# Attention and a squared-ReLU feed-forward on one core: all engines in written order, weight rounding in single hops, value products in one run

## The chip, the cores and the metric

The kernel runs on one core of one Trainium2 chip. The metric is the device time of one execution in microseconds (us). Five runs of the kernel before gave 1637.34 to 1641.2 us, median 1638.19. A core has TensorE (PE; its weight loads are shown as PEld), VectorE (DVE), ScalarE (ACT), GpSimd (POOL) and SyncE (SP), which here only issues transfers. Each has an instruction stream of its own.

## What is computed

```python
# q, k, v: (8, 12, 448, 64) float32; w_in (768, 2048), w_out (2048, 768): 64-bit floats
def rmsnorm(x, g):
    return x / np.sqrt(np.mean(x * x, axis=-1, keepdims=True) + 1e-06) * g
scores = np.matmul(rmsnorm(q, g_q), rmsnorm(k, g_k).transpose(0, 1, 3, 2)) / np.sqrt(64)
attn = softmax(scores)                      # row maximum taken off, sums plus 1e-09
x = np.matmul(attn, v)                      # then (B,H,S,D) -> (3584, 768)
g = np.maximum(x @ w_in, 0.0) ** 2
out = g @ w_out                             # (3584, 768) float32
```

## The kernel before

The program looks at the gains first: if the scores can't grow large, it takes `attention_then_ffn_bounded`, which needs no row maximum. Only that branch runs on these inputs and only it is spoken of.

**Attention.** Two heads of one batch make a *pair*; there are 8 x 6 = 48. The 448 rows of a head are cut into NJ = 4 chunks of SP = 112. For a pair i, `load` and `load_v` bring q, k and v; `norm` squares on ScalarE, sums on DVE, then takes the root's inverse (the power, L535) and scales (L537) on POOL into `qkn`; `transposes` turns `qkn` on TensorE into two PSUM tiles `pt`, which ScalarE copies into `qkT` with the gains; `scores` computes one chunk of scores transposed (`sc`) and its exp on ScalarE (`pr`); `values` multiplies chunks of `pr` with v into `pav`, and `sums` multiplies `pr`, or with `pe_sums` off the sum `acc` of the four chunks, with ones into `tot`; `finish` takes the reciprocal of `tot` (L601) and writes `pav` times it into `xT` (L602). For the second batch of a span it also makes the differences `xC` (L607 to L612).

**Feed-forward.** Two batches are one *span*; there are four. Each of the two products of a span is done by seven products of half-size blocks in place of eight (Strassen's way in Winograd's form): the weights' blocks A11, A12, A22 and their combinations S1 to S4 lie ready in DRAM (`w1s`, `w2s`), the data's combinations are made on DVE: `xC` in `finish`, `gC` in `combine` (four subtractions for each of HF = 8 values f). `first_product` goes through f = 0..7; each f has seven *units* (yields) of one half-size product, accumulated in the PSUM tiles `pa`, `pb`, `pc`, `pd` and added up on DVE (`z`, `y`, `g22`, `g21`, `g12`), with ReLU on ScalarE and the square on POOL or ScalarE (`activate`). `second_product` yields after each matmul; a group of eight fills a PSUM tile `ps`, which DVE adds up into `p1`, `y`, `ct`; `deliver` transposes a finished `ct` into `po`, and ScalarE and SP bring it out.

**Weights.** They arrive as 64-bit floats and are turned to 32 bits in the kernel, 32 chunks of 128x768 (n = 0..31, half for each matrix), two making the seven blocks of one f. `make_w(n, step)` has four steps: 0, exponent on DVE (L451) and two Relus on ScalarE (L453, L454); 1, sign (L457), mask (L458) and low word (L459) on DVE, then a Copy on ScalarE (L460); 2, two products on POOL (L467) and for an odd n the four combinations (L471 to L474); 3, for an odd n the blocks are written to DRAM. Raw words and blocks lie in the buffers of `gC` and in parts of `gT` and of a spare pool, which the data needs later. `weights(upto)` makes whole *ticks*: in tick n, step 0 of chunk n, step 1 of n - 1, step 2 of n - 2 and step 3 of n - 3, all issued at one place, and then the loads of raw chunks whose place is free.

**Order.** The main part runs: attention of span 0 with 14 ticks spread over it; first product of span 0 with ticks to 29; attention of ALONE = 3 pairs of span 1 with the last ticks; `combine` for all f; then for each span its second product, interleaved with the attention of the next span (its remaining pairs), and the next first product. `attention` has two places per pair where other work is put in (yields): the values of a pair are split, chunks 0 and 1 behind its own scores 2 and 3, chunks 2 and 3 behind scores 0 and 1 of the next pair, where `finish` stands as well. The last line of the listing's branch says who sets the order: TensorE and SP execute in written order, while DVE, ScalarE and POOL get an order from a planner at build time.

**PSUM.** `ps_s` has two tiles of two banks (`sc`), `ps_o` one each of `o` (`pav`) and `t` (`tot`, and `pa`), `ps_m` two (`pt`, `pb`, `pc`, `pd`, `ps`, `po`).

Of the kernel before, what the change touches and what calls it, by code (L numbers as in the profile page):

```python
# [9 lines left out]
F32 = mybir.dt.float32  # L10
# [294 lines left out]
def attention_then_ffn_bounded(  # L305
# [132 lines left out]
    def make_w(n, step):  # L438

        if not 0 <= n < 2 * NFC:  # L440
            return
        b = [blocks_of(n)[:, i] for i in range(8)]

        at = (S2, A22)[n % 2]
        e = blocks_of(n)[:, at:at + 2].rearrange("p k m -> p (k m)")
        eu = e.bitcast(U32)
        words = words_of(n)
        low, high = pairs_of(words)
        f = low.bitcast(F32)
        if step == 0 and doubles:  # L450
            nc.vector.tensor_scalar(eu, high, 20, 0x7FF, ALU.logical_shift_right, ALU.bitwise_and)  # L451

            nc.scalar.activation(e, eu, AF.Relu, bias=clamp1, scale=-1.0)  # L453
            nc.scalar.activation(eu, e, AF.Relu, bias=clamp2, scale=-(2.0 ** 23))  # L454
        if step == 1 and doubles:

            nc.vector.scalar_tensor_tensor(eu, high, 0x80000000, eu, ALU.bitwise_and, ALU.bitwise_or)  # L457
            nc.vector.tensor_scalar(high, high, 0xFFFFF, None, ALU.bitwise_and)  # L458
            nc.vector.scalar_tensor_tensor(f, low, 2.0 ** -32, high, ALU.mult, ALU.add)  # L459
            nc.scalar.activation(f, f, AF.Copy, bias=1.0, scale=2.0 ** -20)  # L460
        if step == 2:

            to = ((A11, A12), (A21, A22)) if n < NFC else ((A11, A21), (A12, A22))
            for half, blk in enumerate(to[n % 2]):
                part = slice(half * HW, (half + 1) * HW)
                if doubles:
                    nc.gpsimd.tensor_tensor(b[blk], f[:, part], e[:, part], ALU.mult)  # L467
                else:
                    nc.gpsimd.tensor_copy(b[blk], words.bitcast(F32)[:, part])
        if step == 2 and n % 2:  # L470
            nc.gpsimd.tensor_tensor(b[S1], b[A21], b[A22], ALU.add)  # L471
            nc.gpsimd.tensor_tensor(b[S2], b[S1], b[A11], ALU.subtract)
            nc.gpsimd.tensor_tensor(b[S3], b[A11], b[A21], ALU.subtract)
            nc.gpsimd.tensor_tensor(b[S4], b[A12], b[S2], ALU.subtract)  # L474
        if step == 3 and n % 2:
# [8 lines left out]
            written[0] = n + 1  # L484

    written = [0]
# [22 lines left out]

    qks, vs, qkTs, probs, pavs, tots, accs, normed = {}, {}, {}, {}, {}, {}, {}, {}  # L510
# [14 lines left out]
    def norm(i):  # L525
# [8 lines left out]
        nc.gpsimd.tensor_scalar(rflat, rflat, 1.0 / D, 1e-6, ALU.mult, ALU.add)  # L534
# [9 lines left out]
    def transposes(i):  # L544
        qkn = normed.pop(i)
        qkT = loads.tile([P, 2, S], F32, tag="qkT", name="qkT")
        for s in range(2):
            pt = ps_m.tile([P, S], F32, tag="m", name="pt")
            for j in range(NJ):
                nc.tensor.transpose(pt[:, j * SP:(j + 1) * SP],  # L550
                                    qkn[:, s, j].rearrange("p h d -> p (h d)"), ident[:SP, :SP])
            nc.scalar.activation(qkT[:, s], pt, AF.Copy, scale=gains[:, s:s + 1])  # L552
        qkTs[i] = qkT

    def scores(work, i, c, pe_sums):
# [10 lines left out]
        if c == 0 or pe_sums:  # L566
            pass
        elif c == 1:
            accs[i] = work.tile([SP, 2, S], F32, tag="acc", name="acc", bufs=1)
            nc.gpsimd.tensor_tensor(accs[i], probs[i, 0], pr, ALU.add)  # L570
        else:
            (nc.vector if c == 2 else nc.gpsimd).tensor_tensor(accs[i], accs[i], pr, ALU.add)
# [3 lines left out]
    def values(i, cs, pe_sums):  # L576
        if 0 in cs:
            pavs[i] = ps_o.tile([P, S], F32, tag="o", name="pav")
        for c in cs:
# [6 lines left out]
        if not pe_sums and NJ - 1 in cs:  # L586
# [8 lines left out]
    def finish(work, i):  # L595


        b, hp = divmod(i, NPAIR)
        t = b % 2
        rec = work.tile([P, S], F32, tag="rec", name="rec", bufs=1)  # L600
        nc.vector.reciprocal(rec, tots.pop(i))  # L601
        nc.vector.tensor_tensor(xT[:, t, hp], pavs.pop(i), rec, ALU.mult)  # L602
        del vs[i]
        if t:
# [9 lines left out]
    def attention(work, first, end, pe_sums):  # L614

        last = (first // (2 * NPAIR) + 1) * 2 * NPAIR
        for i in range(first, end):
            if i + 3 < min(last + 2, B * NPAIR):
                load(i + 3)
            scores(work, i, 0, pe_sums)  # L620
            scores(work, i, 1, pe_sums)
            if i + 2 < last:
                norm(i + 2)
            if i > first:
                values(i - 1, (2, 3), pe_sums)
                finish(work, i - 1)
            yield
# [4 lines left out]
            scores(work, i, 2, pe_sums)  # L632
            scores(work, i, 3, pe_sums)
            values(i, (0, 1), pe_sums)
            if i == end - 1:
                values(i, (2, 3), pe_sums)
                finish(work, i)
            yield


    def combine(f):
# [5 lines left out]
        sub(gC[:, 0, f], g12, g11, ALU.subtract)  # L647
        sub(gC[:, 1, f], g22, gC[:, 0, f], ALU.subtract)
        sub(gC[:, 2, f], g21, gC[:, 1, f], ALU.subtract)
        sub(g12, g22, g12, ALU.subtract)  # L650

    def first_product(work, span):
# [11 lines left out]
        def activate(g, src):  # L664
            nc.scalar.activation(g, src, AF.Relu)  # L665
            if span == 0 and src is not g:
# [4 lines left out]
        for f in range(HF):  # L671
# [4 lines left out]
            pa = ps_o.tile([P, S], F32, tag="t", name="pa")  # L676
# [242 lines left out]
```

## Time and profile before

| | us |
|---|---|
| five runs, median (lowest to highest) | 1638.19 (1637.34 to 1641.2) |
| the profiled execution | 1633.54 |
| its span, first to last instruction | 1631.7 |
| first attention: first scores to last sums | 18.3 to 198.6 |
| first product of span 0, to the end of its matmuls | to 334.4 |
| three pairs alone, to the first matmul of the second product | to 386.28 |

Busy times by these stretches, of PE, PEld, DVE, ACT and POOL (number of instructions), then the granted TensorE clock, the share of the DMA engines and GB/s:

```profile
18.30:198.60 180.30, 142.41 (x664) 55.88 (x664) 119.75 (x107) 105.72 (x130) 135.12 (x109) 0.91 0.51 159
198.60:334.40 135.80, 131.35 (x344) 65.35 (x344) 76.62 (x94) 59.89 (x87) 84.62 (x78) 0.97 0.74 241
334.40:386.30 51.90, 39.62 (x178) 15.37 (x177) 36.79 (x40) 26.04 (x34) 42.74 (x33) 0.87 0.58 180
386.30:600.00 213.70, 204.11 (x743) 92.32 (x741) 81.86 (x86) 54.19 (x73) 84.47 (x50) 1.00 0.28 82
600.00:1631.70 1031.70, 999.86 (x3240) 478.31 (x3240) 319.86 (x398) 225.28 (x334) 317.47 (x232) 1.00 0.30 88
```

Some groups of instructions, with their count, busy time, mean ns of one, and the idle time of the engine before them with what ended most of it:

```profile
L601 DVE RECIPROCAL rec<-tot 128x448 f32<-128x448 f32 x48 | 141.9, 2956 | 231.8 <-PE tot L593 231.8
L535 POOL TENSOR_TENSOR rstd<-rstd,mhalf 112x16 f32<-112x16 f32 x48 | 140.5, 2927 | 3.8
L582 PE MATMUL pav<-pr,vt 112*64 112x448 f32 x768 | 179.6, 576 | 41.1 <-issue 33.7
L570 POOL TENSOR_TENSOR acc<-pr 112x896 f32<-112x896 f32 x33 | 68.5, 2076 | 86.6 <-PE tot L593 79.3
```

A timeline row gives start, duration, engine, line, operation, output and inputs, shape and count; in brackets stands the engine's idle time before it and what ended it.

### The profile page before, as it was taken

How to read it: one execution, taken by the hardware profiler on the slowest of the kernel's cores; microseconds unless marked ns; L12 is line 12 of the kernel's file. 1: busy time of each engine (PE TensorE's matmuls, PEld its weight loads, DVE VectorE, ACT ScalarE, POOL GpSimd, SP SyncE). 2: the span in 40 equal slices, each digit the busy share in tenths (PEclk: the TensorE clock that was granted, in tenths of full speed). 3: DMA queues.
4: the chain of work that ended last, by engine and by line, in shares of the span. 5: the costliest groups of instructions: out<-in, count | busy, mean ns of one | idle time of the engine just before them, and what ended most of it. 6: DMA issues, size and time to landing. Idle time of an engine off the chain costs nothing.

```text
span 1631.7 us, 14479 instructions
## 1 busy us (share of the span) xinstructions
PE 1519.3 (93%) x5172; PEld 708.6 (43%) x5172; DVE 638.1 (39%) x729; ACT 475.8 (29%) x661; POOL 672.1 (41%) x516
## 2 busy tenths in 40 slices
PE   4688799978999999999999999999999999999998
PEld 2233354533444445554444445554444445555444
DVE  4556846576333333333333332333333342332001
ACT  5456435463232311123233311123332311211000
POOL 5967737685434402235554421225555320221000
PEclk9799899989999999999999999999999999999999
DMA  5345367864232233333232313333233213333332
GB/s 170 108 150 187 121 225 261 249 216 126 74 96 85 79 88 89 98 88 96 85 90 81 100 56 99 88 96 97 85 90 92 71 56 91 87 87 95 102 105 63
DMA packets 157717, 180.37 MB, mean 111 GB/s; under 512 B 10692, under 2 KB 134084, under 8 KB 157636
## 3 DMA queue, kind: packets, MB, share of 16 engines
q1 hardware_dynamic: 157636, 179.35, 36.4%
q8 instruction: 43, 0.70, 0.2%
q14 instruction: 38, 0.31, 0.1%
HBM read 146.28 MB, written 33.03 MB: 110 GB/s over the span
## 4 chain that ended last, share of the span: by engine, by line
PE 82%; DVE 5%; POOL 3%; ACT 3%; issue 3%; DMA 3%; SPq 1%; DVEq 0%; POOLq 0%; ACTq 0%
PE ps L733 31%; PE sc L561 8%; PE pav L582 8%; PE pa L661 8%; PE pd L661 8%; PE pc L661 8%; PE pb L661 4%; PE tot L593 4%; PE pt L550 2%; ACT qkT L552 1%; DMA words<-in_moe_w_out_dram 1%; DMA qk<-in_k_dram 1%; POOL gC L467 1%; DVE ct L747 1%; POOL qkn L537 1%
## 5 line engine op out<-in xcount | busy, mean ns | idle before, releaser
L733 PE MATMUL ps<-gT,sw 128*128 128x448 f32 x768 | 306.6, 547 | 7.1 <-DVE ct L747 3.6
L669 POOL TENSOR_TENSOR gT<-gT 128x448 f32<-128x448 f32 x120 | 115.2, 960 | 376.1 <-ACT gT L665 376.1
L733 PE MATMUL ps<-gC,sw 128*128 128x448 f32 x576 | 230.6, 546 | 4.0 <-ACT osb L725 2.0
L601 DVE RECIPROCAL rec<-tot 128x448 f32<-128x448 f32 x48 | 141.9, 2956 | 231.8 <-PE tot L593 231.8
L564 ACT ACTIVATE pr<-sc 112x896 f32<-112x896 f32 x192 | 166.8, 914 | 191.3 <-PE sc L561 191.3
L582 PE MATMUL pav<-pr,vt 112*64 112x448 f32 x768 | 179.6, 576 | 41.1 <-issue 33.7
L733 PEld LDWEIGHTS ps<-gT,sw 128*128 128x128 f32 x768 | 141.0, 190 | 157.2 <-issue 141.4
L561 PE MATMUL sc<-qkT 64*112 64x448 f32 x768 | 173.6, 570 | 7.8 <-ACT pr L564 7.1
L661 PE MATMUL pa<-xT,sw 128*128 128x448 f32 x384 | 157.2, 546 | 3.0 <-DVE rec L601 3.0
L733 PEld LDWEIGHTS ps<-gC,sw 128*128 128x128 f32 x576 | 106.1, 190 | 118.3 <-issue 110.5
L535 POOL TENSOR_TENSOR rstd<-rstd,mhalf 112x16 f32<-112x16 f32 x48 | 140.5, 2927 | 3.8
L665 ACT ACTIVATE gT<-gT 128x448 f32<-128x448 f32 x96 | 55.1, 575 | 291.6 <-DVE gT L693 183.1
L534 POOL TENSOR_SCALAR rstd<-rstd 112x16 f32<-112x16 f32 x48 | 32.6, 680 | 242.0 <-DVE rstd L533 241.1
L582 PEld LDWEIGHTS pav<-pr,vt 112*64 112x64 f32 x768 | 50.8, 143 | 153.8 <-issue 147.6
L552 ACT ACTIVATE qkT<-pt,gains 128x448 f32<-128x448 f32 x96 | 58.7, 632 | 170.9 <-PE pt L550 170.9
L725 ACT COPY osb<-po 112x512 f32<-112x512 f32 x48 | 28.1, 586 | 275.5 <-PE po L723 275.5
L661 PEld LDWEIGHTS pa<-xT,sw 128*128 128x128 f32 x384 | 73.4, 192 | 74.6 <-issue 70.6
L537 POOL TENSOR_TENSOR qkn<-qk,rstd 112x512 f32<-112x512 f32 x96 | 103.5, 1100 | 3.6
L570 POOL TENSOR_TENSOR acc<-pr 112x896 f32<-112x896 f32 x33 | 68.5, 2076 | 86.6 <-PE tot L593 79.3
L533 DVE TENSOR_REDUCE rstd<-qkn 112x16 f32<-112x1024 f32 x48 | 58.1, 1211 | 115.8 <-ACT qkn L530 115.6
L561 PEld LDWEIGHTS sc<-qkT 64*112 64x112 f32 x768 | 61.4, 174 | 89.0 <-issue 65.3
L550 PE MATMUL pt<-ident,qkn 112*128 112x112 f32 x384 | 53.7, 271 | 37.2 <-ACT qkT L552 16.7
(82 smaller groups left out, 1650.6 us busy)
## 6 DMA issues: line engine op xcount, KB each, us to landing
sw<-w1s SPq DMA_DIRECT2D x224, 192.0 KB, 2.4
sw<-w2s SPq DMA_DIRECT2D x168, 256.0 KB, 2.7
qk<-in_q_dram SPq DMA_DIRECT2D x48, 224.0 KB, 3.2
qk<-in_k_dram SPq DMA_DIRECT2D x48, 224.0 KB, 3.7
vt<-in_v_dram SPq DMA_DIRECT2D x48, 224.0 KB, 3.0
w1s<-gC SPq DMA_DIRECT2D x8, 1344.0 KB, 6.2
w2s<-gC SPq DMA_DIRECT2D x24, 448.0 KB, 4.6
out_dram<-osb SPq DMA_DIRECT2D x48, 224.0 KB, 2.9
```

The costliest lines, as they stand in the source:

```text
L535: nc.gpsimd.tensor_tensor(rflat, rflat, mhalf, ALU.pow)
L537: nc.gpsimd.tensor_tensor(qkn[:, s].rearrange("p j h d -> p h j d"), qk[:, s].rearrange("p h (j d) -> p h j d", d=D), rstd[:, s].rearrange ...
L550: nc.tensor.transpose(pt[:, j * SP:(j + 1) * SP], qkn[:, s, j].rearrange("p h d -> p (h d)"), ident[:SP, :SP])
L552: nc.scalar.activation(qkT[:, s], pt, AF.Copy, scale=gains[:, s:s + 1])
L561: nc.tensor.matmul(sc[:, h, 0:S], qkT[rows, 1, c * SP:(c + 1) * SP], qkT[rows, 0, :], start=True, stop=True)
L564: nc.scalar.activation(pr, sc[:, :, 0:S], AF.Exp)
L570: nc.gpsimd.tensor_tensor(accs[i], probs[i, 0], pr, ALU.add)
L582: nc.tensor.matmul(pavs[i][h * D:(h + 1) * D, :], vs[i][:, h, c, :], pr[:, h, :], start=(c == 0), stop=(c == NJ - 1))
L601: nc.vector.reciprocal(rec, tots.pop(i))
L661: nc.tensor.matmul(ps, stream[n][:, c], rhs[:, c], start=first and c == 0, stop=c == HC - 1, skip_group_check=not first)
L669: nc.gpsimd.tensor_tensor(g, g, g, ALU.mult)
L733: nc.tensor.matmul(ps, stream[n][:, c % 4], rhs_of[i][:, c], start=c == 0, stop=c == HF - 1)
```

## The change

All engines now run in written order. What was left to the planner is written out:

- `make_w` becomes a generator `prepare(t)` that gives one *hop* at each step, four hops to a tick. Hop 0: sign of chunk t - 1 on DVE, first product of t - 2 on POOL. Hop 1: mask and low word of t - 1, second product of t - 2, S1. Hop 2: Copy of t - 1 on ScalarE, exponent of chunk t on DVE, S2 and S3. Hop 3: the two Relus of chunk t, S4, the write-back of chunk t - 3, and the loads of raw words. `weights(upto)` counts hops.
- Attention that runs alone yields once per pair instead of twice. EARLY, LATE and ALL are 48, 120 and 140 hops: 12 ticks in the first attention (four hops at each pair's yield), 18 in the first product of span 0, 5 in the attention alone, which has ALONE = 2 pairs instead of 3.
- All values of a pair stand in one run behind its scores 2 and 3, and `finish` right behind them. The subtractions of `xC` are a function of their own, `combine_x`, placed in the next pair behind its `norm`. In alone attention, ScalarE's copies of the transposes stand behind the exps (`take_transposes`). Both `pt` tiles are taken before the transposes.
- The sums of probabilities (`acc`) are all on DVE; the scale-add of `norm` moves from POOL to DVE; constants are set on DVE.
- `pa` moves from `ps_o` to `ps_s`; in span 0 the square of `g21` moves to ScalarE; in later spans `combine` of f - 1 is done in two parts between the units of f.
- Only two raw chunks, instead of five, are loaded at the start.

```diff
+    def prepare(t):
...
+        if there(t - 1) and doubles:
+            b, e, eu, low, f, high = parts(t - 1)
+            nc.vector.scalar_tensor_tensor(eu, high, 0x80000000, eu, ALU.bitwise_and, ALU.bitwise_or)
+        if there(t - 2):
+            value(t - 2, 0)
+        yield
+        if there(t - 1) and doubles:
+            nc.vector.tensor_scalar(high, high, 0xFFFFF, None, ALU.bitwise_and)
+            nc.vector.scalar_tensor_tensor(f, low, 2.0 ** -32, high, ALU.mult, ALU.add)
+        if there(t - 2):
+            value(t - 2, 1)
+        total(t - 2, S1, A21, A22, ALU.add)
+        yield
+        if there(t - 1) and doubles:
+            nc.scalar.activation(f, f, AF.Copy, bias=1.0, scale=2.0 ** -20)
+        if there(t) and doubles:
+            b, e, eu, low, f, high = parts(t)
             nc.vector.tensor_scalar(eu, high, 20, 0x7FF, ALU.logical_shift_right, ALU.bitwise_and)
+        total(t - 2, S2, S1, A11, ALU.subtract)
+        total(t - 2, S3, A11, A21, ALU.subtract)
+        yield
+        if there(t) and doubles:
             nc.scalar.activation(e, eu, AF.Relu, bias=clamp1, scale=-1.0)
             nc.scalar.activation(eu, e, AF.Relu, bias=clamp2, scale=-(2.0 ** 23))
...
+        total(t - 2, S4, A12, S2, ALU.subtract)
+        n = t - 3
+        if there(n) and n % 2:
...
+        while loaded[0] <= t + 2 and all(
+                place_of(m) != place_of(loaded[0]) for m in range(max(t - 1, 0), loaded[0])):
+            load_w(loaded[0])
+            loaded[0] += 1
+        yield
...
-        nc.gpsimd.tensor_scalar(rflat, rflat, 1.0 / D, 1e-6, ALU.mult, ALU.add)
+        nc.vector.tensor_scalar(rflat, rflat, 1.0 / D, 1e-6, ALU.mult, ALU.add)
...
+        pts[i] = [ps_m.tile([P, S], F32, tag="m", name="pt") for _ in range(2)]
+        for s, pt in enumerate(pts[i]):
...
+    def take_transposes(i):
+        qkTs[i] = loads.tile([P, 2, S], F32, tag="qkT", name="qkT")
+        for s, pt in enumerate(pts.pop(i)):
+            nc.scalar.activation(qkTs[i][:, s], pt, AF.Copy, scale=gains[:, s:s + 1])
...
+        if c and not pe_sums:
+            nc.vector.tensor_tensor(accs[i], probs[i, 0] if c == 1 else accs[i], pr, ALU.add)
...
-    def attention(work, first, end, pe_sums):
+    def attention(work, first, end, alone):
...
             if i + 2 < last:
                 norm(i + 2)
             if i > first:
-                values(i - 1, (2, 3), pe_sums)
-                finish(work, i - 1)
-            yield
+                combine_x(i - 1)
+            if not alone:
+                yield
             if i + 1 < B * NPAIR:
                 load_v(i + 1)
             if i + 1 < last:
                 transposes(i + 1)
-            scores(work, i, 2, pe_sums)
-            scores(work, i, 3, pe_sums)
-            values(i, (0, 1), pe_sums)
+                if not alone:
+                    take_transposes(i + 1)
+            scores(work, i, 2, alone)
+            scores(work, i, 3, alone)
+            if alone:
+                if i + 1 < last:
+                    take_transposes(i + 1)
+                yield
+            values(i, alone)
+            finish(work, i)
             if i == end - 1:
-                values(i, (2, 3), pe_sums)
-                finish(work, i)
-            yield
+                combine_x(i)
+            if not alone:
+                yield
...
-            pa = ps_o.tile([P, S], F32, tag="t", name="pa")
+            pa = ps_s.tile([P, 2, 512], F32, tag="s", name="pa")[:, 0, 0:S]
...
-    ALONE = 3
-    EARLY, LATE, ALL = 14, 29, 2 * NFC + 3
+    ALONE = 2
+    EARLY, LATE, ALL = 4 * 12, 4 * 30, 4 * (2 * NFC + 3)
...
-        for n in range(WORDS):
-            load_w(n)
+        for _ in range(2):
+            load_w(loaded[0])
+            loaded[0] += 1
...
-                weights(EARLY * (u + 1) // (4 * NPAIR))
+                weights(EARLY * (u + 1) // (2 * NPAIR))
...
-        with tc.manual_schedule(engines={mybir.EngineType.PE, mybir.EngineType.SP}):
+        with tc.manual_schedule():
```

## The prediction

> **What bounds the kernel now.** I read the page's busy shares and its slices first, then the busy time by stretches, then the chain of waits and the timeline inside the stretches where TensorE idles.
>
> ```profile
> span 1631.7 us, 14479 instructions
> ...
> PE 1519.3 (93%) x5172; PEld 708.6 (43%) x5172; DVE 638.1 (39%) x729; ACT 475.8 (29%) x661; POOL 672.1 (41%) x516
> ...
> PE   4688799978999999999999999999999999999998
> ...
> PEclk9799899989999999999999999999999999999999
> ```
>
> TensorE sets the time, and it is full from about the tenth of 40 slices on. What can be won lies in front of that. By stretches (PE, PEld, DVE, ACT, POOL busy, then clock, DMA share, GB/s):
>
> ```profile
> 0.00:100.00 100.00, 62.73 (x282) 25.00 (x283) 53.47 (x52) 53.12 (x65) 72.48 (x67) 0.90 0.43 132
> 100.00:200.00 100.00, 81.61 (x394) 32.22 (x392) 70.90 (x63) 57.26 (x71) 71.60 (x60) 0.93 0.52 167
> 200.00:300.00 100.00, 97.85 (x251) 48.64 (x252) 57.23 (x71) 43.81 (x63) 60.44 (x56) 0.97 0.70 232
> 300.00:400.00 100.00, 86.50 (x319) 38.59 (x318) 68.48 (x83) 47.46 (x65) 68.22 (x56) 0.93 0.64 198
> 400.00:500.00 100.00, 95.59 (x357) 42.55 (x356) 29.88 (x28) 27.37 (x36) 47.65 (x29) 1.00 0.31 90
> ```
>
> The loss is in the first 400 us, the only part with weights to round: stage A, the first attention (first scores at 18.3, last sums end at 198.6), stage B, the first product of span 0 (to 334.4), and stage C, the attention alone (first matmul of the second product at 386.28). From there TensorE is 95% busy or more (stage D). In A a typical idle stretch reads so in the timeline:
>
> ```profile
> 171.06 0.92 PE L593 MATMUL tot<-pr,ones 112*64 112x448 f32 x4
> ...
> 172.19 2.95 DVE L601 RECIPROCAL rec<-tot 128x448 f32<-128x448 f32 x1
> ...
> 175.23 1.22 DVE L533 TENSOR_REDUCE rstd<-qkn 112x16 f32<-112x1024 f32 x1
> ...
> 176.37 0.61 DVE L602 TENSOR_TENSOR xT<-pav,rec 128x448 f32<-128x448 f32 x1
> ...
> 177.08 1.76 PE L582 MATMUL pav<-pr,vt 112*64 112x448 f32 x4 [2.50 <-issue]
> ```
>
> The sums end, DVE takes 2.95 + 0.61 us (here with a reduce of the norm between), and only then is the single `pav` buffer free; in between TensorE has the transposes (0.98) and two scores (1.76), so it idles 2.50 us. "issue" hides the true releaser, xT. All such gaps in A from 18.3 on add up to 37.8 us. Without its gap a pair takes 10.68 us (values at 150.94 and 163.90 are 12.96 apart, gap 2.28; 163.90 to 177.08 gives 13.18 - 2.50). Twelve pairs are 128 us, A lasts 180.3, so some 14 us more are matmuls at a low clock behind gaps (1.76 us for four values where 0.92 is usual).
>
> Stage C hangs on POOL and the write-back of weights:
>
> ```profile
> 376.01 1.73 SPq L481 DMA_DIRECT2D w2s<-gC  x3
> ...
> 382.04 1.16 DVE L647 TENSOR_TENSOR gC<-gT 128x448 f32<-128x448 f32 x2 [5.41 <-DMA w2s<-gC]
> ...
> 385.65 1.73 ACT L564 ACTIVATE pr<-sc 112x896 f32<-112x896 f32 x2 [11.09 <-PE sc L561]
> ...
> 386.28 6.28 PE L733 MATMUL ps<-gT,sw 128*128 128x448 f32 x16
> ```
>
> The last weights leave at 376.01, DVE may overwrite gC from 382.04 (combine), and the second product starts at 386.28, 51.9 after the first product's end.
>
> **The change, stage by stage.**
>
> **A.** Values in one run put scores 0 and 1 (1.76), transposes (0.98) and scores 2 and 3 (1.76) = 4.5 us of TensorE work between the last sums and the next values, where DVE needs 2.95 + 0.61 and two crossings, 3.8. The gap of 2.0 to 3.4 us goes, if nothing else is late. What could be late is the loop that written order ties together: ScalarE's exp 0, exp 1 and Square (0.91 + 0.91 + 1.05), DVE's reduce 1.2 and the small scale-add moved from POOL (0.2 there; I take 0.2), then combine_x, then the hops: sign 1.08, mask 0.9, add 1.25, next exponent 0.75 (means by form from 20 to 200 us, 4.0 together), ScalarE's Copy behind the add and two Relus (0.92 + 1.87), then the next exp 0. Sum with crossings: 10.5. combine_x adds one subtraction (1.0 under POOL's load) in pairs 7 to 9 and three in pairs 10 and 11: 11.5 and 13.5. POOL has per pair 2.97 (power) + 2.45 + 2.26, and 4.4 more every second pair: 9.9 on the mean. So pairs take the longer of 10.7 and this loop: first pair 12.7 as now, six at 11.1 (0.4 for what doesn't overlap), three at 11.7, two at 13.4 = 141; I add 4 for loads of raw weights, which land in 6 to 7 us here. A ends at about 163.5: **-35**. Ends: all eleven later pairs at 10.68 and no wait for loads give -50; the hops at the worst durations of the stage (1.5, 1.3, 1.66, 1.2: 5.7) give 12.2, 13.2, 15.2 a pair and -20; with every second pair another 1 us late at POOL, -14. The twelve ticks replace fourteen in A, so two move to B. On SP the loads and write-backs of hop 3 wait for POOL work one pair older, and qk's loads behind them have a pair of lead: nothing, as long as POOL is under 10.7 a pair. The start doesn't move: constants set by DVE instead of POOL, and gains behind the first norm, all lie before 7.48 us, when the first qk lands, and TensorE's first work at 15.65 waits for POOL's qkn as now; two raw chunks now load ahead of qk(2), which waits for its buffer until 16.5 in any case.
>
> The clock: the stretch from 75 to 80 us shows 0.50 after gaps of 2.56 and 1.99 us, yet after 2.28 us at 163.90 it stays 1.00. Pairs 10 and 11 keep a gap of 2.7 each, which I price by these rows at up to 1.2 us of slow matmuls each; they are counted within the 4 us above. The Trainium skill's "TensorE: Matmul & The Clock Gate" (Part 1) has the half clock come after an idle window of about 3.4 us; by it such gaps would cost nothing beyond themselves, and the sum would be 2 us lower.
>
> **B.** 56 units at 2.2536 us are 126.2; B took 135.8, of it 3.05 waiting for the reciprocal of pair 11 (`pa` shared its buffer with `tot`) and about 3 of low clock. `pa` moves to `ps_s`: the first product starts at once, only `pb`'s third part waits for xC (reciprocal 2.95 + 0.61 + 0.61 against 3.75 of work): 0.7. Transposes in the middle keep 1.3. Eighteen ticks instead of fifteen, nine hops to seven units: two hops fall on units 3 and 6, and where they are exponent and sign, DVE waits for two Relus (1.87) and is then late for z, which must be there one unit (2.25) later. By hand that is two places of about 2 us less some slack: 3. One square for each f of span 0 moves from POOL (0.96) to ScalarE (0.58, idle half of the time between 200 and 300 us): nothing. B: 131.2, **-4.6**; ends -7 (no late z) and +6 (a 2 us wait at every second f and on each of four late loads).
>
> **C.** Two pairs alone instead of three, but five ticks in two lumps. I walk it by hand with the durations of the rows, from B's end E: the Relus of chunk 29 hold exp 0 of pair 12 to E+5; norm, then POOL 2.9 + 2.1 until E+13.6; only then value(28), and SP may load chunk 31 (E+16, lands E+22); DVE's sign for it ends E+27, and in written order the reciprocal of pair 12 stands behind it (E+30.7), the norm of pair 15 behind that, POOL's value(31) and totals behind that (E+43.6); write-back lands E+48.5 (4.8 as now). Queued behind it on DVE are now all 32 subtractions of combine (0.535 apart, 17.1), and behind those the sums of probabilities of pair 14, which TensorE needs: it resumes its dense stream at E+71. Before, TensorE at E+71 (405.4) was ahead of this by ten matmuls of the second product (7.5), a pair's transposes, scores and half its values (5.9) and two scores (1.8): 15.2. **+15**. Ends: +22 if that late load and the write-back each take 3 to 4 us more, +5 if two thirds of combine's 17 us find other TensorE work beside them.
>
> **D.** The probability sums move from POOL (2.08) to DVE (1.08 each, three a pair); reciprocal and combine_x stand before product sums. DVE: 2.95 + 0.61 + 3.24 + 1.4 + 1.2 + 1.1 = 10.5 of the 19.4 us that a pair takes. The cover is DVE's idle time (9.11 before a reciprocal at 756.49); without it each late sum holds a `ps_m` buffer and so the next transposes. In the two pairs per span with three subtractions I find 0.3 to 1.2 us: +2; the wait for POOL's sum at each span's end (0.6, three times) goes: -1. **+1**; ends -2 and +20 (0.6 in each of 34 pairs). In spans 1 to 3 combine in two pieces lies beside 2.25 us units with DVE a third busy: nothing.
>
> **Sum** on the profiled execution (1633.5, span 1631.7): -35 - 4.6 + 15 + 1 = -23.6, 1609.9. The median shown is 1638.2, 4.7 above it: 1638.2 - 23.6 = 1614.6, so 1614.
>
> **Rivals.**
> Combine hides: C costs 2 instead of 15, as DVE's subtractions of free regions run early and TensorE has work. For it: before, some ran at 346 us. Against: written order starts with gC's first region, where the last chunk lies. 1601.
> Rounding binds: DVE and ScalarE hops at their contended worst, A -20.4, B +5, C +15, D +1, +0.6 in all: 1639. For it: DVE and POOL both at 71% in A now. Also here: that the scheduler's order was the written one, which the Relus of rounding between exps at 156 to 163 us speak against.
> Slower: in D the sums queue behind reciprocal or norm, and transposes, which take both `ps_m` buffers, wait. From 0.7 us in each of 34 pairs the gain is used up; at 2 us late less 0.7 slack, 34 x 1.3 = 44: 1658. For it: one buffer held by an unfinished product already costs 0.72 at the transposes of most pairs. Against: DVE's 9 us of slack.
>
> **How the numbers follow.** Forecast 0.55, own range 1603 to 1627; combine hides 0.15; rounding binds 0.16 (0.06 faster, 0.05 the same, 0.05 slower); slower 0.14. Faster 0.76, same 0.05, slower 0.19, at 0.2% (3.3 us), what this measurement can tell. The range 1592 to 1645 takes in the first three and leaves out most of the last and a low tail.
>
> **What would show it.** A: gaps before `pav` under 1 us, pairs 11 to 12 apart, last sums near 163. B: about 131 long, no wait on rec. C: the second product's first matmul 45 to 52 us behind B's end, then an idle TensorE of some 10 us before `tot`, released by DVE's sums behind combine. D: pairs still 19.4 apart. It is wrong if A's pairs stay at 13 or more, or if transposes in D wait on DVE.

## The result, and the profile after

The changed kernel takes 1641.85 us (median of 24 runs, 1636.98 to 1645.3), the kernel before on the same chips 1638.24 (44 runs, 1634.33 to 1644.62): ratio 1.0017, 95% interval 1.0009 to 1.0025. That is 0.17% slower, within the 0.2% that the prediction calls the same; the forecast was 24 us faster. Behind it stand a large gain and three losses. The page of the profiled execution: span, busy shares, and the rows of TensorE and of its granted clock in 40 slices.

```profile
span 1642.4 us, 14375 instructions
...
PE 1513.1 (92%) x5160; PEld 709.5 (43%) x5160; DVE 728.4 (44%) x849; ACT 484.6 (30%) x669; POOL 520.4 (32%) x391
...
PE   6999897748999999999999999989999999999998
...
PEclk9999999868999999999999999999999999999999
```

TensorE now runs nearly full from the second slice on, and has its hole in slices 7 to 9 (246 to 370 us). By stretches (PE, PEld, DVE, ACT, POOL busy, then clock, DMA share, GB/s), with the stages of the prediction as borders:

```profile
18.30:151.80 133.50, 129.11 (x665) 51.63 (x666) 99.41 (x96) 92.97 (x115) 105.87 (x75) 0.99 0.59 180
151.80:310.70 158.90, 134.62 (x346) 65.89 (x348) 106.79 (x119) 77.50 (x111) 111.97 (x89) 0.95 0.68 226
310.70:365.07 54.37, 28.18 (x121) 10.28 (x121) 26.71 (x29) 22.91 (x29) 32.91 (x26) 0.74 0.48 152
365.07:605.30 240.23, 224.14 (x809) 102.86 (x810) 112.72 (x125) 58.55 (x77) 41.26 (x24) 0.97 0.27 79
605.30:1642.40 1037.10, 994.90 (x3217) 477.27 (x3215) 378.82 (x471) 228.03 (x334) 220.67 (x168) 0.99 0.30 87
```

A table that all runs below share, read from the timelines. "A end" is the end of the first attention's sums; B runs from there to the end of span 0's first product; "B to P1" from there to the start of span 1's first product, so it holds the pairs alone, `combine` and the second product of span 0 (a longer stretch than the prediction's C, and all that follows of it); P1 and P2 are the first products of spans 1 and 2. Times are in us; those marked * were timed once, the others are medians of rounds. The stage columns come from one profiled execution each. x11 and x13 are the same kernel, and their B differs by 1.8 us, so a difference of that size shows nothing.

| kernel | time | A end | B | B to P1 | P1 | P2 |
|---|---|---|---|---|---|---|
| before | 1638.2 | 198.6 | 136.0 | 272.9 | 127.9 | 127.9 |
| after | 1641.9 | 151.8 | 158.9 | 294.6 | 135.4 | 134.3 |
| x1_planner | 1630.6 | 175.9 | 142.4 | 282.2 | 127.9 | 127.9 |
| x2_before_written * | 1736.9 | 223.7 | 156.9 | 304.4 | 135.7 | 135.6 |
| x3_load_late | 1626.8 | 151.6 | 155.5 | 294.4 | 127.9 | 127.9 |
| x4_values_split * | 1683.6 | 191.7 | 161.6 | 290.4 | 135.6 | 134.4 |
| x5_z_hops * | 1649.6 | 151.4 | 175.6 | 297.9 | 127.9 | 127.9 |
| x6_t_first * | 1623.5 | 151.6 | 151.9 | 294.3 | 127.9 | 127.9 |
| x7_combine_spread * | 1622.6 | 151.7 | 155.5 | 291.1 | 127.9 | 127.9 |
| x8_alone3 * | 1618.4 | 151.4 | 157.2 | 284.8 | 127.9 | 127.9 |
| x9_exp_early * | 1619.2 | 155.8 | 147.8 | 291.4 | 127.9 | 127.9 |
| x10_fewer_ticks * | 1625.6 | 165.2 | 136.4 | 298.9 | 127.9 | 127.9 |
| x11_all4 * | 1609.0 | 151.3 | 151.9 | 281.0 | 127.9 | 127.9 |
| x12_all5 | 1614.9 | 156.5 | 148.7 | 284.5 | 127.9 | 127.9 |
| x13_all4_again | 1611.2 | 151.1 | 153.7 | 280.9 | 127.9 | 127.9 |
| x14_all4_15ticks | 1623.2 | 151.2 | 140.1 | 305.5 | 127.9 | 127.9 |

After against before: A -46.8, B +22.9, B to P1 +21.7, P1 and P2 +7.5 and +6.4, the two later second products -0.5 each: +10.7, the difference of the two profiled spans (1642.4 - 1631.7). The medians differ by less, 3.6: the profiled execution of before was a quick one (1633.5 us) and that of after one of its slower ones (1644.2).

**A** is what was hoped for. In this timeline (start, duration, engine, line, operation, tiles, shapes, count; idle time before in brackets) the sums end at 72.8 and `xT` at 76.5. Meanwhile TensorE has scores, transposes and again scores (1.76 + 1.25 + 1.76), and the next values show no bracket at all:

```profile
72.87 2.96 DVE L638 RECIPROCAL rec<-tot 128x448 f32<-128x448 f32 x1 [1.27 <-PE tot L632]
...
75.87 0.62 DVE L639 TENSOR_TENSOR xT<-pav,rec 128x448 f32<-128x448 f32 x1
...
77.32 0.97 PE L621 MATMUL pav<-pr,vt 112*64 112x448 f32 x4
```

**B** shows one tick of rounding in front of a sum that TensorE needs. VectorE stands 3.03 us at the sign step, because in written order it must wait there for ScalarE's second Relu; then come mask and low word, and only then `z`, for which `pd` has waited 2.88:

```profile
172.58 0.94 ACT L493 ACTIVATE gC<-gC,clamp 128x768 uint32<-128x768 f32 x1
...
173.55 0.96 DVE L471 SCALAR_TENSOR_TENSOR gC<-words,gC 128x768 uint32<-128x768 uint32 x1 [3.03 <-ACT gC L493]
...
174.62 1.18 DVE L476 TENSOR_SCALAR words<-words 128x768 uint32<-128x768 uint32 x1
...
175.84 1.65 DVE L477 SCALAR_TENSOR_TENSOR words<-words 128x768 f32<-128x768 uint32 x1
...
177.41 0.61 DVE L736 TENSOR_TENSOR z<-p,pb 128x448 f32<-128x448 f32 x1
...
178.07 2.15 PE L713 MATMUL pd<-xT,sw 128*128 128x448 f32 x5 [2.88 <-DVE z L736]
```

That is one of five late `z`. In B of the changed kernel TensorE idles 24.3 us, where the same list for before holds 4.4; the three longest of its waits (us in total, times, longest one):

```profile
PE pd L713 <- DVE z L736: 13.3, 5, 5.2
...
PE pb L713 <- ACT qkT L596: 7.8, 1, 7.8
...
PE pd L713 <- DMA sw<-w1s: 2.2, 1, 2.2
```

The largest single gap is the second of these: at the last f the copies of the transposes (L596) stand behind a Relu, that one behind an exponent, and the exponent waits for a late load of raw words.

```profile
290.24 1.38 DVE L486 TENSOR_SCALAR gC<-words 128x768 uint32<-128x768 uint32 x1 [2.94 <-DMA words<-in_moe_w_out_dram]
...
293.46 1.14 ACT L596 ACTIVATE qkT<-pt,gains 128x448 f32<-128x448 f32 x2
...
294.13 1.12 PE L713 MATMUL pb<-xC,sw 128*128 128x448 f32 x1 [7.81 <-ACT qkT L596]
```

**C**: the last weights leave at 355.42, `combine` starts when they have landed (361.32), the second product waits for its own weights, and after one run of matmuls TensorE waits for a sum of probabilities, which stands behind all 32 subtractions. Within the two pairs alone it has idled 14.1 us before (gaps of 2.76, 7.95 and 3.42, behind exps and `xT`):

```profile
355.42 1.72 SPq L502 DMA_DIRECT2D w2s<-gC  x3
...
361.32 0.63 DVE L698 TENSOR_TENSOR gC<-gT 128x448 f32<-128x448 f32 x1 [6.34 <-DMA w2s<-gC]
...
365.07 8.58 PE L789 MATMUL ps<-gT,sw 128*128 128x448 f32 x14 [12.07 <-DMA sw<-w2s]
...
380.50 1.09 DVE L612 TENSOR_TENSOR acc<-pr 112x896 f32<-112x896 f32 x1
...
385.17 1.76 PE L632 MATMUL tot<-acc,ones 112*64 112x448 f32 x4 [4.90 <-DVE acc L612]
```

**D** lost where nothing was priced. In the first product of spans 1 and 2 the load of `qk` stands on SP until POOL has scaled the old one into `qkn`; the weights' loads are queued behind it:

```profile
692.62 2.17 POOL L578 TENSOR_TENSOR qkn<-qk,rstd 112x512 f32<-112x512 f32 x2
...
694.81 0.33 SPq L557 DMA_DIRECT2D qk<-in_q_dram  x1
...
695.74 9.29 SPq L546 DMA_DIRECT2D sw<-w1s  x6
...
699.86 4.82 PE L713 MATMUL pd<-xC,sw 128*128 128x448 f32 x6 [4.32 <-DMA sw<-w1s]
```

4.32 us of gap, and 4.82 for six matmuls that take 2.42 elsewhere. Before, the line stood at the same place on SP, but the planner had run that pair's norm ahead of the product: its trace has rows of POOL's scaling (L537) at 562 and 563 us and none from there to 690, and the load goes out at 686.97 with nothing waiting for it:

```profile
561.89 2.04 POOL L537 TENSOR_TENSOR qkn<-qk,rstd 112x512 f32<-112x512 f32 x2
...
686.97 0.42 SPq L516 DMA_DIRECT2D qk<-in_q_dram  x1
```

### The profile page after: what moved, and what is told of

It reads as the page before. It is cut to its first block, busy times and chain, and to the rows that moved or that the text cites. A ratio compares the mean times of both kernels' runs of the same rounds, so it can differ in the third digit from the quotient of the medians.

```text
span 1642.4 us, 14375 instructions
## 1 busy us (share of the span) xinstructions
PE 1513.1 (92%) x5160; PEld 709.5 (43%) x5160; DVE 728.4 (44%) x849; ACT 484.6 (30%) x669; POOL 520.4 (32%) x391
## 4 chain that ended last, share of the span: by engine, by line
PE 77%; DVE 7%; POOL 6%; ACT 4%; issue 4%; DMA 2%; SPq 1%; POOLq 0%; DVEq 0%; ACTq 0%
PE ps L789 31%; PE sc L604 8%; PE pav L621 8%; PE pd L713 7%; PE pc L713 7%; PE pa L713 6%; PE tot L632 4%; PE pb L713 3%; PE pt L590 2%; POOL gC L459 2%; POOL gC L466 2%; POOL rstd L576 1%; DVE acc L612 1%; ACT qkT L596 1%; POOL qkn L578 1%
## 5 line engine op out<-in xcount | busy, mean ns | idle before, releaser
L789 PE MATMUL ps<-gT,sw 128*128 128x448 f32 x768 | 312.1, 555 | 21.6 <-DMA sw<-w2s 12.1
L576 POOL TENSOR_TENSOR rstd<-rstd,mhalf 112x16 f32<-112x16 f32 x48 | 150.0, 3126 | 443.3 <-DVE rstd L575 416.7
L721 POOL TENSOR_TENSOR gT<-gT 128x448 f32<-128x448 f32 x112 | 112.8, 1007 | 519.9 <-ACT gT L717 519.9
L604 PE MATMUL sc<-qkT 64*112 64x448 f32 x768 | 174.4, 574 | 14.0 <-ACT pr L607 13.3
L621 PE MATMUL pav<-pr,vt 112*64 112x448 f32 x768 | 164.6, 553 | 3.4 <-DVE xT L639 3.4
L612 DVE TENSOR_TENSOR acc<-acc,pr 112x896 f32<-112x896 f32 x68 | 78.8, 1159 | 140.6 <-ACT pr L607 137.1
L578 POOL TENSOR_TENSOR qkn<-qk,rstd 112x512 f32<-112x512 f32 x96 | 104.8, 1113 | 3.8
L596 ACT ACTIVATE qkT<-pt,gains 128x448 f32<-128x448 f32 x96 | 58.8, 636 | 133.8 <-PE pt L590 133.8
L612 DVE TENSOR_TENSOR acc<-pr 112x896 f32<-112x896 f32 x34 | 37.1, 1092 | 131.6 <-ACT pr L607 131.6
L713 PE MATMUL pd<-xT,sw 128*128 128x448 f32 x192 | 80.0, 554 | 13.3 <-DVE z L736 13.3
L713 PE MATMUL pd<-xC,sw 128*128 128x448 f32 x192 | 81.6, 563 | 11.4 <-DMA sw<-w1s 10.9
```

The source lines that it names most:

```text
L576: nc.gpsimd.tensor_tensor(rflat, rflat, mhalf, ALU.pow)
L578: nc.gpsimd.tensor_tensor(qkn[:, s].rearrange("p j h d -> p h j d"), qk[:, s].rearrange("p h (j d) -> p h j d", d=D), rstd[:, s].rearrange ...
L596: nc.scalar.activation(qkTs[i][:, s], pt, AF.Copy, scale=gains[:, s:s + 1])
L604: nc.tensor.matmul(sc[:, h, 0:S], qkT[rows, 1, c * SP:(c + 1) * SP], qkT[rows, 0, :], start=True, stop=True)
L612: nc.vector.tensor_tensor(accs[i], probs[i, 0] if c == 1 else accs[i], pr, ALU.add)
L621: nc.tensor.matmul(pavs[i][h * D:(h + 1) * D, :], vs[i][:, h, c, :], pr[:, h, :], start=(c == 0), stop=(c == NJ - 1))
```

## Experiments: order and structure apart

**x1_planner**: the new structure, with the planner's order for VectorE, ScalarE and POOL again.

```diff
-        with tc.manual_schedule():
+        with tc.manual_schedule(engines={mybir.EngineType.PE, mybir.EngineType.SP}):
```

> The changed program, but DVE, ScalarE and POOL get the planner's order again; TensorE and SP stay in written order. Theory 1 (written order gives the gain of the first attention back: product sums stand behind rounding hops and a norm in the first product of span 0, which takes 160.9 us instead of 135.8): the first attention still ends near 151 to 160, that first product falls to 134 to 142, the first products of spans 1 and 2 to 127 to 130, the whole to 1605 to 1622. Rival (the work that was moved out of the attention, 18 ticks instead of 15 and two pairs alone, is paid there in any order): that product stays at 155 or more and the whole at 1633 to 1645.

1630.57 us, ratio 0.9942 (0.992 to 0.9964), between the two. The planner loses 24 us in A (175.9, where 151 to 160 was expected, for 151.8) and 4.8 in the two later second products (251.3 and 250.3 for 248.5 each); it wins 16.5 in B, 12.4 from B to P1 and 14 in P1 and P2. So the written order isn't bad as such: it is worth 29 us in two parts and costs 43 in three.

**x2_before_written**: the old structure in written order, as in the diff above with its signs turned round, on the kernel before.

> The program before, only with all engines in written order. Theory 1: whole ticks of four steps in one place put up to 4 us of DVE work and ScalarE's Relus in front of product sums and exps, so the first attention gets longer than 180 us and the first product longer than 150; whole 1660 to 1720. Rival (written order itself costs nothing, only the new places of the hops do): within 5 us of the program before.

1736.86, over the range expected. The same order that gains 24 us on the new structure loses 25 in A on the old one (223.7 for 198.6). Order and structure can't be priced apart.

**x4_values_split**: the changed kernel, with the values of a pair in A and in the pairs alone split again over two pairs (in written order as after).

```diff
+                if alone:
+                    values(i - 1, alone, (2, 3))
+                    finish(work, i - 1)
...
-            values(i, alone)
-            finish(work, i)
+            if alone:
+                values(i, alone, (0, 1))
...
```

> The changed program, but in attention that runs alone the values of a pair are split again in two halves, the second behind scores 0 and 1 of the next pair, with the reciprocal behind it. Theory: the run of values is what hides the reciprocal and the product into xT (3.8 us) behind 4.5 us of scores and transposes, so pairs of the first attention go back from 10.7 to 12.7 to 13.5 and the attention ends at 172 to 185; whole 1655 to 1675. Rival (pairs got shorter because hops in written order no longer interrupt exps): pairs stay under 11.3, whole within 5 us of 1642.

1683.6: A ends 39.9 us later, with a gap in front of the first run of values of every pair but the first again (eleven gaps, 32.9 us together), the longest of them this:

```profile
143.93 1.76 PE L622 MATMUL pav<-pr,vt 112*64 112x448 f32 x4 [4.96 <-issue]
```

The one run of values is worth more than was expected, since a split pair pays for the gap, and for slow matmuls behind it (1.76 for four where 0.97 is usual; TensorE is busy for 139.8 us in A, where the changed kernel has 129.3).

## Experiments: the loss in D

**x3_load_late**: the load behind the next norm, one f later.

```diff
         if u == 7 * (HF - 3):
             norm(nxt)
-            load(nxt + 2)
         if u == 7 * (HF - 2):
+            load(nxt + 2)
             norm(nxt + 1)
```

> The changed program; in the first products the load of qk two pairs ahead is issued before the second norm (unit 42) instead of behind the first (unit 35). Theory: SP waits there for POOL's qkn to free the buffer, and the w1s loads queue behind it (TensorE idle 4.3 us and 2.4 us of low clock in each of spans 1 and 2, 2.2 us and part of the low clock in span 0). So the first products of spans 1 and 2 fall from 134.8 and 133.7 to 127.5, the whole by 12 to 18 us to 1624 to 1630. Rival (the w1s loads are late by DMA traffic): no change, or the wait moves to the new place; 1638 to 1645.

1626.78, ratio 0.9924 (0.9902 to 0.9946). P1 and P2 are 127.9 again, B is 3.4 shorter. The same stretch, without a bracket:

```profile
689.42 2.42 PE L713 MATMUL pa<-xT,sw 128*128 128x448 f32 x6
...
691.68 2.42 PE L713 MATMUL pd<-xC,sw 128*128 128x448 f32 x6
...
696.80 0.38 SPq L557 DMA_DIRECT2D qk<-in_q_dram  x1
```

One moved line is the whole of D's loss. All runs below are on this kernel.

## Experiments: the loss in B

**x5_z_hops**: the hops of each f put where no `z` follows, in clumps of two or three behind units 1, 3, 4 and 5.

```diff
-                weights(EARLY + (LATE - EARLY) * (u + 1) // N1)
+                weights(EARLY + 9 * (u // 7) + (0, 2, 2, 5, 7, 9, 9)[u % 7])
```

> The late load of x3, and in the first product of span 0 the nine hops of each f stand only behind units 1, 3, 4 and 5 (2, 3, 2, 2), none between unit 6 and the next z. Theory (z, which frees the PSUM buffer of the third next unit, stands behind up to three hops of DVE work that wait for ScalarE's Relus): the waits for z (2.9, 1.6, 1.4 and part of 5.2 and 2.3 us) and the low clock behind them go, and so do most of the 7.8 us at the transposes, since no Relu stands before their copies; that product falls from 155.5 to 134 to 142, the whole to 1603 to 1613. Rival (eighteen ticks are too much work for this stage, POOL at 80%, whatever the places): the waits move to other sums, 150 or more, whole 1620 or more.

1649.6, B 175.6. The theory that only `z` is late fell: `z` is late once now (1.4 us), but g12 is at five f, behind the same wait at the sign step, and holds the buffer of the next `pc`.

```profile
174.23 0.96 DVE L471 SCALAR_TENSOR_TENSOR gC<-words,gC 128x768 uint32<-128x768 uint32 x1 [3.04 <-ACT gC L493]
...
175.77 1.81 PE L713 MATMUL pc<-xC,sw 128*128 128x448 f32 x2 [2.01 <-DVE gT L760]
```

The list of waits in B has for it:

```profile
PE pc L713 <- DVE gT L760: 13.3, 5, 4.1
```

**x6_t_first**: the copies of the transposes in front of the hops.

```diff
-                weights(EARLY + (LATE - EARLY) * (u + 1) // N1)
                 ahead(u, start_of(1))
+                weights(EARLY + (LATE - EARLY) * (u + 1) // N1)
```

> The late load of x3, and in the first product of span 0 norms, loads and transposes are placed in front of a unit's hops instead of behind them. Theory (the copies of the transposes stand behind two Relus, which wait for an exponent, which waits for a load of raw words; both PSUM buffers are held): the 7.8 us at unit 49 and 2.4 us of low clock go, 155.5 falls to 144 to 148. The late z stays. Rival (POOL's norm is late for the transposes): 155 or more.

1623.5; B -3.6, less than expected, and only twice what B varies by between x11 and x13. Most of the gap of 7.81 had gone with x3's load already (3.67 there, 3.15 now), since the raw words that it began with stood behind that load on SP; of the rest, a late `z` at the f before shrinks from 3.94 to 2.59.

**x9_exp_early**: exponent and Relus two hops earlier.

```diff
             nc.vector.scalar_tensor_tensor(eu, high, 0x80000000, eu, ALU.bitwise_and, ALU.bitwise_or)
+        if there(t) and doubles:
+            b, e, eu, low, f, high = parts(t)
+            nc.vector.tensor_scalar(eu, high, 20, 0x7FF, ALU.logical_shift_right, ALU.bitwise_and)
...
             nc.vector.scalar_tensor_tensor(f, low, 2.0 ** -32, high, ALU.mult, ALU.add)
+        if there(t) and doubles:
+            e, eu = parts(t)[1:3]
+            nc.scalar.activation(e, eu, AF.Relu, bias=clamp1, scale=-1.0)
+            nc.scalar.activation(eu, e, AF.Relu, bias=clamp2, scale=-(2.0 ** 23))
...
```

> The kernel of x3 with the exponent step (VectorE) of a tick moved from its third hop to its first and the two Relus (ScalarE) from the fourth to the second, so that the sign step in the next tick's first hop comes three hops behind the Relus and not one. Theory (in first product of span 0 VectorE stands 1.4 to 3.0 us in each tick at the sign step for ScalarE's Relus, and everything written behind it, z, g21 and g12, is late by that): that wait is gone, the stretch from the last sums to the last first product falls from 155.5 to 138 to 147 us, and the time from 1626 to 1609 to 1619. Rival (VectorE's hops are long in themselves beside POOL, and the sums are late because of their length): the stretch stays at 150 to 158, the time at 1621 to 1629.

1619.2. In the changed kernel's stage B, VectorE's idle time before the sign step, and how often:

```profile
  ACT gC L493: 26.1, 13
```

In x3, from which x9 departs, the same line says 27.6 in 13; in x9 the list that held it is empty. Of that wait removed, B gained 7.7, and A lost 4.2. So the wait was real, but not all of it was on TensorE's path. That the hops behind it are long themselves, as the rival said, fits this and is not shown apart.

**x10_fewer_ticks**: 15 ticks in B as before the change, two more in A and one more in the pairs alone.

```diff
-    EARLY, LATE, ALL = 4 * 12, 4 * 30, 4 * (2 * NFC + 3)
+    EARLY, LATE, ALL = 4 * 14, 4 * 29, 4 * (2 * NFC + 3)
```

> The kernel of x3 with 15 ticks of rounding in the first product of span 0 instead of 18, as before the change had: two more ticks in the first attention, one more in the two pairs alone. Theory (how many hops lie in the product sets its length): the stretch with the product falls from 155.5 by 3/18 of its excess over 127.9, 4 to 7 us, the first attention grows by 0 to 5 and the pairs alone by 2 to 5, so the time stays within 4 us of 1626. Rival (each wait is from the order inside a tick, but ticks cost nothing elsewhere): the time falls to 1618 to 1622.

1625.6: the time stays, but for other sizes than expected (4 to 7 us in B, 0 to 5 in A). B falls by 19.1 to 136.4, what it was before the change, A grows by 13.6, B to P1 by 4.5. With 14 ticks the hops no longer come four to a pair in A, so the 13.6 hold the number of ticks and their new places together. Its stage B, by the same columns as above:

```profile
165.20:301.60 136.40, 130.25 (x348) 64.79 (x346) 94.11 (x107) 71.61 (x104) 99.48 (x79) 0.99 0.70 229
```

## Experiments: the loss in C, and all together

**x7_combine_spread**: half of `combine` behind the first two places of the second product.

```diff
-    for f in range(HF):
+    for f in range(HF // 2):
         combine(f)
...
+                    if span == 0 and u < 2:
+                        combine(HF // 2 + 2 * u)
+                        combine(HF // 2 + 2 * u + 1)
```

> The late load of x3, and only half of combine stands in front of the second product of span 0; two f each stand behind the first two yields of the next attention. Theory (the sums of probabilities of the first pair stand behind all 32 subtractions): the 4.9 us at tot and the low clock behind them go, the time from the end of the first product to the next one falls from 294.4 to 286 to 290. Rival (the product's third group then waits for combine): 293 or more.

1622.6; B to P1 -3.3, short of the 4 to 8 expected, and the wait in front of `tot` goes from 5.18 in x3 to 3.86.

**x8_alone3**: `ALONE = 3`, as before the change.

> The late load of x3, with three pairs alone instead of two. Theory (the second product can't start before the last weights are written, about 54 us behind the first product, and TensorE idles 12 us there, so a third pair alone costs only its longer sums, 2.3 us): the first matmul of the second product stays within 3 us of 54, the time to the next first product falls from 294.4 to 284 to 289. Rival (the third pair's norm and hops push POOL's last weights back by as much): 293 to 300.

1618.4; B to P1 -9.6, as expected. The third pair is work for TensorE while the last chunks are rounded and written.

**x11_all4**, timed again as **x13_all4_again**: x3, x6, x7 and x8 together.

> x3, x6, x7 and x8 together: load one place later, the transposes' copies written ahead of the hops, half of the combination behind the first two places of the second product, three pairs alone. If they add up: 1626.8 - 3.3 - 4.2 - 8.4 = 1611; if x7 and x8 cover the same idle time (the stretch between the first product's end and the next span's): 1613 to 1617. Above 1618 one of them takes back what another gains.

> The kernel of x11, timed in rounds. If x11's single time stands: 1606 to 1612, ratio to before 0.980 to 0.985, and under x12 by 3 to 7 us. If the 1609 was a low one: 1612 to 1617, equal to x12.

1609.03 and then 1611.22 in rounds, ratio 0.983 (0.9802 to 0.9859): the parts add up (1611 by their sum), and this version beats both kernels.

**x12_all5**: that, with x9's order of hops.

> The kernel of x11 with the exponent step and the Relus of x9 two hops earlier. If VectorE's wait for ScalarE's Relus is a cost of its own beside the four others, the product of span 0 (151.9 us from the last sums to its end in x11) falls by 4 to 8 and the time from 1609 to 1602 to 1606, against 1638 before; if x6 and x9 take away the same wait, it stays within 2 us of 1609.

1614.89, ratio 0.9858 (0.9834 to 0.9883): a miss, 3.7 us slower than x13, though the intervals of the two ratios overlap. B gained 5.0, but A ended 5.4 later and B to P1 grew by 3.6. In A the transposes wait for POOL's `qkn` twice, 1.84 and 2.84 us, where x13 has one such wait of 1.34; why POOL is later there was not taken apart.

**x14_all4_15ticks**: x13 with `LATE` at `4 * 27`: 12 ticks in A, 15 in B, 8 beside the three pairs alone.

> The kernel of x11 with 15 ticks of rounding in the first product of span 0 (as before the change) in place of 18, and eight in place of five beside the three pairs alone; the first attention keeps its twelve. Theory (the product's excess is the three ticks more, wherever they begin): from the last sums to the product's end 134 to 141 us instead of 151.9, as in x10, with the first attention's end still near 151; the stretch from there to the next span's product grows by 5 to 15 (281 to 286 to 296), as 12 more hops fall on three pairs, so the time is 1600 to 1612. Rival (in x10 it was where the ticks began against the units, 14 for 12, and not their number): the product stays at 148 to 153.

1623.19, ratio 0.9903 (0.9878 to 0.9929). With A as in x13, B is 140.1: the number of ticks counts, not where they begin. But B to P1 grows by 24.6, over what was expected, for the hops now stand in front of the exps of the pairs alone (TensorE waits 2.55, 7.59 and 12.03 us for these exps, in x13 2.74 once). TensorE behind the longest of them:

```profile
345.53 1.71 ACT L607 ACTIVATE pr<-sc 112x896 f32<-112x896 f32 x2
...
346.48 3.33 PE L604 MATMUL sc<-qkT 64*112 64x448 f32 x8 [12.03 <-ACT pr L607]
```

## Why the prediction was wrong

**Its main view held**: the loss of before was the single `pav` buffer in A, and one run of values removes it. The size of A was off: -35 forecast, -46.8 measured. The mis-sized term is the loop of hops, walked at 11.1 to 11.7 us for nine pairs. The pairs' sums end 10.46 apart (nine of eleven steps between 10.46 and 10.72) with no gap of TensorE's in these nine; only two steps are long, 12.50 and 13.86. That is 7.3 of the 11.8 us; 4 more are the waits for loads of raw words, which did not come. The two ticks that left A carry more than was said: x10 puts them back, at new places, for 13.6 us.

**B is the step that failed**: "By hand that is two places of about 2 us less some slack: 3", and the sum of -4.6 with ends of -7 and +6. It came out at +22.9. The walk took one order of hops on two units and asked how late `z` is there. In its place the trace shows `z` late at five f of eight (13.3 us), 7.8 us lost at the transposes' copies and 2.2 for a load, where nothing was put; and TensorE's busy time is 134.6 for 127.5 of matmuls and transposes in the forecast, at a mean clock of 0.95. The walk had the wait for two Relus at two places; VectorE stood at the sign step in thirteen ticks (26.1 us). And freeing `z` alone makes other sums late (x5). Number of ticks and order work together:

| B, us | planner's order | written order |
|---|---|---|
| 15 ticks | 136.0 (before, old structure) | 136.4 (x10), 140.1 (x14) |
| 18 ticks | 142.4 (x1) | 158.9 (after), 155.5 (x3) |

At 18 ticks the written order costs 16.5 us (158.9 against 142.4), and by hand three ticks cost 12 to 19 (151.9 to 153.7 in x11 and x13 against 140.1, 155.5 against 136.4). What they cost the planner, 6 by the table, is not shown, since before has the old structure too; and that structure, with its 15 ticks of four steps at one place, takes 156.9 in written order (x2). So neither the number of ticks nor the order sets B alone. The prediction counted the two ticks that left A and the one that left C as moved, and priced their arrival at nothing beyond that one `z`. Two smaller parts show as well: the load of D's kind (3.4, x3; the wait of 2.2 is gone there) and the place of the transposes' copies (3.6, x6), both near the 1.8 by which B varies.

**C**: forecast +15 with ends of +5 and +22; B to P1 shows +21.7. The walk by hand held nearly in its points: write-back landed 50.6 us behind B's end (48.5 forecast), TensorE went on 74.5 behind it (71), and the second product began at 54.4, beyond its 45 to 52. `combine` took 19.2 where 17.1 was put. The walk names no idle time before the second product, which waits 12.07 for its weights; the idle time before `tot` was 4.90, not 10. The two choices behind it are x8's third pair (9.6) and x7's half of `combine` (3.3); the rest isn't taken apart.

**D**: +1 forecast, +13.9 in P1 and P2 measured, and none of it on the named path: the second products even took 0.5 less each, so VectorE has the room that was claimed for the sums. Missing was the queue of SP. The line didn't move, and the text looked only at the queues past which a step was moved; but with POOL no longer ahead, the load waits, and the weights behind it.

**The rivals.** "Combine hides" falls with C. "Slower", sums behind the reciprocal in D, falls with the second products. "Rounding binds" named 1639 and has the right work, but put its loss in A (-20.4 there), which gained 46.8, and only +5 in B; that its total is near the measured one is luck, the sum of opposite errors. It is luck too that 1641.85 lies inside the wide range of 1592 to 1645. Of the prediction's own signs, "about 131 long" for B is the one that failed most clearly.

**In short**: 47 us were won in A, and 23, 22 and 14 given back. x3, x6, x7 and x8 win some 30 of them again.

## What to carry to other kernels

Before an engine is taken from a planner, list for every queue what the planner had run early: each such instruction can be a wait in written order, and here one line on the queue that also issues the loads for TensorE cost 15 us. Background work has a price for each unit of it that differs by stage (here 6.8 us a tick in A by x10, with its new places; 3.9 to 6.4 in B and 4.5 to 8.2 from B to P1 by x10 and x14), so shifting it between stages won nothing: x10 gives back what it wins in B, and x14 gives back more. Try the planner with the new structure as well as the written order with it; here each was better in other stages.

## What was not expected of the hardware

VectorE's steps of one tick are longer in B than in A. The low word (two inputs) of the chunks in `words`, in A and in B of the changed kernel, as lowest, median and highest ns:

```profile
L477 DVE SCALAR_TENSOR_TENSOR words<-words x4: 958/960/964, 70.2 to 137.6; 128x768 f32<-128x768 uint32 x4
...
L477 DVE SCALAR_TENSOR_TENSOR words<-words x8: 959/1651/1659, 175.8 to 302.8; 128x768 f32<-128x768 uint32 x8
```

The four steps together take 3.5 us a tick in A and 4.5 in B (means over all chunks); the prediction had 4.0, from A of before. Over all chunks of A and B the low word has two lengths: fifteen times 1.57 to 1.67 us, each beside a product, a sum or a scaling on POOL (L459, L466, L578), and fourteen times 0.96, beside none of these (at most POOL's power, L576, or a square, L721). The Trainium skill's "GPSIMD Engine Reference" (1. Specifications) says that GpSimd shares VectorE's way to SBUF and that it contends with VectorE's instructions of two SBUF inputs or in a two-port mode; the step's two lengths, 960 and 1651, agree with that. The sign step (L471) has two inputs too and is no longer in B (1.08 us in the mean) than in A (1.10), which doesn't. No run here separates contention from other causes.

Gaps of 2.6 to 3.2 us slow TensorE in some places: in x1 eight matmuls take 2.64 us behind a gap of 2.79 and 3.33 behind one of 3.16, for 1.76 elsewhere, and in the changed kernel 3.00 behind 2.60. There five others take 2.15 behind 2.88, at a granted clock of 1.00. The first two lines are x1's, the third is the changed kernel's.

```profile
140.41 3.33 PE L604 MATMUL sc<-qkT 64*112 64x448 f32 x8 [3.16 <-ACT pr L607]
...
166.27 2.64 PE L604 MATMUL sc<-qkT 64*112 64x448 f32 x8 [2.79 <-ACT pr L607]
```
```profile
142.19 3.00 PE L604 MATMUL sc<-qkT 64*112 64x448 f32 x8 [2.60 <-ACT pr L607]
```

The idle window of about 3.4 us that the Trainium skill's "TensorE: Matmul & The Clock Gate" (Part 1) gives doesn't tell these cases apart. Behind the gap of 3.16 the slow matmuls cost another 1.57 us (3.33 - 1.76).
